# First stage of a Fourier-convolution block: PSUM tiles by half group instead of by row tile, and nine of sixteen copies on ScalarE

## The chip, the cores and the metric

The kernel runs on one core of one Trainium2 chip. The metric is the device time of one launch in microseconds (us). The engines are named as in the profile: PE (TensorE, matmuls; PEld its weight loads), DVE (VectorE), ACT (ScalarE), POOL (GpSimd), SP (SyncE, which issues DMAs).

## What is computed

One block with two parts. The first is a gated long convolution over 2048 positions and 512 channels, done by a Fourier transform; the second is a small MLP. Cut to what matters:

```python
def _A_ref(q, k, v, shift_k, ssm_k, ssm_D):
    # k_shift: a causal convolution of k with 4 taps per channel
    kv = k_shift * v
    kv_f = rfft(pad(kv, to 2S), along the positions)
    kf_f = rfft(pad(ssm_k, to 2S))
    y = irfft(kv_f * kf_f)[:S]
    y = y + kv * ssm_D
    return q * y

h  = x + _A_ref(layernorm(x), A_k, A_v, shift_k, ssm_k, ssm_D)
h2 = h + relu(layernorm(h) @ w1) @ w2
```

## The kernel before

The program writes its order out by hand: every engine executes its instructions in the order of the source, and waits on semaphores that the framework places between engines.

The transform is split into stages of small matrices. What the case is about is **the first stage**, the function `stage1(fl, B, gb, dmul)`. It is called eight times for the convolution's filter (`kfl` into `BK`, with `dmul=dmask`, lines 373 and 413; called filter groups 0 to 7 here) and eight times for the signal kv (`xfl` into `BX`, line 419; signal groups 0 to 7). Each call is one group:

- TensorE multiplies 64-row weights (a slice of `fl`) with the 64-row tables `f1hi` and `f1lo`, the second accumulating onto the first (L308). There are two row tiles, partitions 0 to 63 and 64 to 127, that hold different channels and run side by side in the array: 8 values of `gi` x 2 tables x 2 row tiles = 32 matmuls, each writing 128 columns, as runs of 32.
- The results go to two PSUM tiles of two banks each (`bank2`). In the kernel before, row tile 0 writes the first and row tile 1 the second, and the matmuls alternate between them.
- The tiles are read out. A filter group does it with two VectorE additions of the mask `dmask` (L320, the `i=0` half of the output, where the convolution's direct term is added) and two ScalarE copies (L323, the `i=1` half); where two engines read the same tile, the second waits for the first. A signal group does it with one copy of a whole tile by ScalarE and one by VectorE (`copy("AD"[rp], ...)`, in the helper's lines L278 and L280).

All these PSUM tiles come from one pool, `psum`, of four buffers that are given out in turn; so a matmul into a new tile waits until the readers of the tile allotted four before it are done. The taps' matmuls (`pkv`, L340, multiplied into `vT` by VectorE, L343), the transposes (`pst`, L291, copied by ScalarE L295 or VectorE L297) and the next stage's products draw from the same pool.

The order of the work around it: four transposing steps of the filter; then for filter groups 0 to 6 the taps of one or two row groups, the group, and some sines on ScalarE (`more_sines`, `ec_sins`); then four transposing steps of kv (`to_rows(vT, h, xfl)`), filter group 7, the eight signal groups, and the next stage, which multiplies both transforms:

```python
FIRST = "u0K +u0 u1K +u1 s0K1 s0X1 u0X s0K2 =u0 u1X =u1 ..."
```

There `u0K` is TensorE's product for one pair of frequencies from `BK` (L456), `+u0` ScalarE's copy of it (`ktu`, L442), `s0K1` and `s0X1` the same for sums, from `BK` and `BX` (`us`, L478), `u0X` the pair from `BX`, into the other half of the PSUM tile that `+u0` has read, and `=u0` VectorE's multiplication (L494). `s0X1` is the first to read `BX`, and reads from all eight signal groups. Then follow the inverse transform (`psi`, L603, whose results L278 and L280 copy too) and the MLP (L706, L722).

Of the kernel before, what the change touches and what calls it, by code (L numbers as in the profile page):

```python
# [9 lines left out]
ALU = mybir.AluOpType  # L10
BF16 = mybir.dt.bfloat16
# [4 lines left out]
P = 128  # L16
# [40 lines left out]
def kernel(  # L57
# [13 lines left out]
    nc = tc.nc  # L71
    _, S, D = A_q.shape
# [4 lines left out]
    DC = D // P  # L77
# [3 lines left out]
    halves = (lo, hi)  # L81
# [9 lines left out]
    early = pl.push("early", side="right")  # L91
# [35 lines left out]
    for dp in range(2):  # L127
        src = bass.AP(tensor=A_ssm_D.tensor, offset=A_ssm_D.offset, ap=[[0, 1], [1, DC * P]])
# [22 lines left out]
    def bank2(name):  # L151
        return psum.tile([P, 2, 512], F32, tag="ps", name=name)[:]
# [18 lines left out]
    f1hi = early.tile([P, 2, 2, 16, 2], BF16, name="f1_hi")  # L171
    f1lo = early.tile([P, 2, 2, 16, 2], BF16, name="f1_lo")
# [44 lines left out]
    for rg in range(DC):  # L217
        rows = slice(32 * rg, 32 * rg + 32)
# [21 lines left out]
    def big_sin(out, turns, scale):  # L240
        nc.scalar.activation(out=out, in_=turns, func=ACT.Sin, scale=scale * TURN / 8192)

    dmask = early.tile([P, 2, 2, 16, 2, DC], BF16, name="dmask")
    nc.gpsimd.memset(dmask[:], 0.0)
    for dp in range(2):
        row = slice(64 * dp, 64 * dp + 1)
        for rp in range(2):
            for sp in range(2):
                src = draw[row, 256 * rp:256 * rp + 256].rearrange("p (r u s l d) -> p r u s l d", r=2, s=2, l=2, d=2)[:, :, :, sp, :, dp]
                for w in range(2):  # L250
                    nc.gpsimd.tensor_copy(out=dmask[row, rp, sp, :, w].rearrange("p u (r l) -> p r u l", l=2), in_=src)

    nc.gpsimd.tensor_scalar(out=r2, in0=r2, scalar1=n2c[:], scalar2=2048.0, op0=ALU.mult, op1=ALU.add)

# [21 lines left out]
    def copy(eng, o, i):  # L276
        if eng == "A":
            nc.scalar.copy(out=o, in_=i)  # L278
        else:
            nc.vector.tensor_copy(out=o, in_=i)  # L280
# [16 lines left out]
                nc.vector.tensor_single_scalar(out=oi, in_=pst.bitcast(I32).rearrange("p b i c -> p b c i"),  # L297
                                               scalar=0, op=ALU.bitwise_or)

    def stage1(fl, B, gb, dmul=None):  # L300

        j, sp = gb // 2, gb % 2
        pss = [bank2("ps1").rearrange("p b (a w r l x) -> p (b a) (w r) l x", a=2, w=2, r=2, l=2) for _ in range(2)]
        for gi in range(8):
            g = 16 * j + 4 * (gi // 2) + 2 * sp + gi % 2
            for f, first in ((f1hi, True), (f1lo, False)):
                for rp, rows in enumerate(halves):
                    nc.tensor.matmul(out=pss[rp][:, gi // 2, :, gi % 2, :],  # L308
                                     lhsT=fl[rows, 2 * g:2 * g + 2, :].rearrange("p d n -> p (d n)"),
                                     rhs=f[rows].rearrange("p w r v h -> p (w r v h)"), start=first, stop=not first,  # L310
                                     tile_position=(64 * rp, 0), skip_group_check=True)
        o = [B.rearrange("p i (u w) (v s) x -> p i u w v s x", w=2, s=2)[:, :, 4 * j:4 * j + 4, :, :, sp, 4 * rp:4 * rp + 4]
             .rearrange("p i u w v x -> p i (u w) v x") for rp in range(2)]
        pv = [p.rearrange("p u (w r) l (v i) -> p i (u w) v (r l)", w=2, i=2) for p in pss]
        if dmul is None:
            for rp in range(2):
                copy("AD"[rp], o[rp], pv[rp])
            return
        for rp in range(2):
            nc.vector.tensor_tensor(out=o[rp][:, 0], in0=pv[rp][:, 0],  # L320
                                    in1=dmul[:, rp, sp, 4 * j:4 * j + 4].rearrange("p u w x -> p (u w) x").unsqueeze(2)
                                    .to_broadcast([P, 8, 16, 4]), op=ALU.add)
            nc.scalar.copy(out=o[1 - rp][:, 1], in_=pv[1 - rp][:, 1])  # L323

    for h in range(4):
        to_rows(sk, h, kfl)
# [38 lines left out]
    for gb in range(7):  # L365
        if gb == 3:
            taps(1, 1, 1, 1)
        elif gb < 6:
            taps(gb // 2, gb % 2)
        else:  # L370
            taps(3, 0)
            taps(3, 1, 1)
        stage1(kfl, BK, gb, dmask)
        if gb < 2:
            more_sines(gb)
        if gb == 1:
            ec_wrap(0)
        if gb in (2, 3, 4, 5):
            ec_sins(0, (gb - 2,))
# [30 lines left out]
    xfl = xkp.tile([P, P, 64], BF16, name="xfl")  # L410
    for h in range(4):
        to_rows(vT, h, xfl[:])
    stage1(kfl, BK, 7, dmask)

    BXt = bxp.tile([P, 32, 66, DC * 2], F32R, tag="X", name="BX")
    BX = BXt[:, :, 2:66, :].rearrange("p g (i k) x -> p i g k x", i=2)
    BXs = BXt[:, :, 0:32, :]
    for gb in range(8):
        stage1(xfl, BX, gb)
    pl.pop("xkp")  # L420
    pl.pop("early")

# [78 lines left out]
    for c in range(8):  # L501
        units, early = {}, {}
        for step in (OTHER if c else FIRST).split():
# [6 lines left out]
            u = step[:2]  # L510
# [296 lines left out]
```

## Time and profile before

| | |
|---|---|
| median of 3 runs | 206.26 us (206.26 to 206.31) |
| profiled execution, its own time | 206.31 us |
| its span, first to last instruction | 204.2 us |
| granted TensorE clock, mean | 0.994 |
| busy share of the span | PE 96%, PEld 67%, DVE 69%, ACT 56%, POOL 39% |
| chain that ended last, by engine | PE 88%, DVE 7%, ACT 2%, issue 1% |
| of it, first-stage matmuls (L308) | 7% of the span |
| taps (L340), next stage (L478, L456) | 5%; 9% and 7% |

A row of the page's groups, or of the timeline, gives line, engine, operation, tiles (written from read), shapes, count, and busy or elapsed time; what stands in brackets in the timeline is how long the engine was idle before and what ended that. "PE" times come from pipelined matmuls, so a busy TensorE need not be at its peak. In the chain of waits each row is a start, a length and the work that the end of the program waited for at that moment; "issue" is time in which the profile shows no reason.

### The profile page before, as it was taken

What the parts mean: (1) busy time and instruction counts of PE and PEld (TensorE: products, weight loads), DVE (VectorE), ACT (ScalarE), POOL (GpSimd) and SP (SyncE); (2) the same over time, 40 slices, a digit from 0 to 9 for tenths busy, and PEclk for the clock granted to TensorE, in tenths of its full rate; (3) what the DMA queues carried; (4) which work ended last, traced back from release to release, by engine and by line L of the source; (5) the groups of instructions that cost most, each with busy time, mean ns of one, the idle gap of its engine ahead of it and who ended that gap; (6) DMA issues with size and microseconds to landing.
All of it is one profiled execution on the core that took longest, in us unless ns stands there. A gap on an engine that the chain in (4) does not pass through costs nothing.

```text
span 204.2 us, 4733 instructions
## 1 busy us (share of the span) xinstructions
PE 195.3 (96%) x1929; PEld 137.2 (67%) x1929; DVE 141.0 (69%) x246; ACT 114.7 (56%) x188; POOL 79.6 (39%) x127
## 2 busy tenths in 40 slices
PE   8899999898999999999999999999999999999991
PEld 2475556887899999899998844475445844444460
DVE  4999888698799998997561967995378660360131
ACT  4987875788578877686880088205940164026300
POOL 7969999960559995212003032062002200002000
PEclk9999999999999999999999999999999999999997
DMA  6999990002600000052636999997643605110011
GB/s 178 337 178 207 176 176 3 3 5 31 248 3 0 3 3 0 22 132 55 106 87 184 207 215 196 171 174 91 91 82 76 135 19 103 32 58 17 0 51 51
DMA packets 47300, 19.94 MB, mean 98 GB/s; under 512 B 42186, under 2 KB 45744, under 8 KB 47280
## 3 DMA queue, kind: packets, MB, share of 16 engines
q1 hardware_dynamic: 43616, 16.14, 41.7%
q10 hardware_dynamic: 3664, 3.51, 6.0%
q8 instruction: 15, 0.25, 0.5%
q14 instruction: 5, 0.04, 0.1%
HBM read 7.02 MB, written 2.10 MB: 45 GB/s over the span
## 4 chain that ended last, share of the span: by engine, by line
PE 88%; DVE 7%; ACT 2%; issue 1%; DVEq 0%
PE ps1m L706 19%; PE ps2m L722 19%; PE psi L603 11%; PE us L478 9%; PE pz L694 7%; PE u L456 7%; PE ps L308 7%; PE pkv L340 5%; PE psz L157 2%; PE pst L291 1%; DVE E L343 1%; DVE BK L320 1%; DVE G L227 1%; DVE E L44 1%; DVE G L225 1%
## 5 line engine op out<-in xcount | busy, mean ns | idle before, releaser
L708 ACT ACTIVATE M<-ps1m 128x512 bf16<-128x512 f32 (+1 forms) x44 | 25.1, 595 | 49.4 <-PE ps1m L706 39.0
L722 PE MATMUL ps2m<-M 128*128 128x512 bf16 (+3 forms) x187 | 38.7, 366 | 0.0
L722 PEld LDWEIGHTS <-M 128*128 128x128 bf16 (+1 forms) x187 | 18.3, 98 | 19.9
L706 PEld LDWEIGHTS <-w 128*128 128x128 bf16 (+1 forms) x176 | 17.4, 100 | 19.9
L565 POOL TENSOR_SCALAR rstd<-mv 128x4 f32<-128x4 f32 x8 | 2.2, 277 | 70.1 <-DVE mv L563 70.1
L402 POOL TENSOR_TENSOR smc<-st 64x256 fp32r<-64x256 f32 x32 | 22.8, 732 | 12.4 <-PE us L478 11.5
L724 DVE SCALAR_TENSOR_TENSOR M<-ps2m,rstd,M 128x512 bf16<-128x512 f32 (+1 forms) x13 | 9.2, 707 | 24.8 <-PE ps2m L722 16.3
L494 DVE TENSOR_TENSOR BK<-u,ktu 128x512 fp32r<-128x512 f32 x32 | 21.2, 685 | 3.5 <-ACT ktu L442 1.9
L603 PE MATMUL psi<-inv,BK 128*128 128x128 f32 x128 | 21.1, 255 | 0.0
L442 ACT COPY ktu<-u 128x512 f32<-128x512 f32 x32 | 18.0, 592 | 5.2 <-PE u L456 4.2
L603 PE MATMUL psi<-inv,BX 128*128 128x256 f32 x64 | 20.5, 337 | 0.0
L603 PEld LDWEIGHTS psi<-inv,BK 128*128 128x128 f32 x128 | 19.7, 197 | 0.0
L706 PE MATMUL ps1m<-M,w 128*128 128x512 bf16 (+1 forms) x88 | 19.3, 379 | 0.0
L706 PE MATMUL ps1m<-xT,w 128*128 128x512 bf16 (+1 forms) x88 | 19.3, 379 | 0.0
L478 PE MATMUL us<-BK,smc 64*128 64x256 f32 x128 | 14.5, 302 | 0.6 <-ACT BX L278 0.6
L456 PE MATMUL u<-BK,st 64*128 64x256 f32 x128 | 13.6, 290 | 0.2 <-DVE BX L494 0.2
L478 PE MATMUL us<-BX,smc 64*128 64x256 f32 x128 | 13.3, 282 | 0.0
L323 ACT CAST BK<-ps 128x512 fp32r<-128x512 f32 x16 | 9.4, 586 | 6.6 <-PE ps L308 4.9
L456 PE MATMUL u<-BX,st 64*128 64x256 f32 x128 | 13.0, 281 | 0.0
L603 PEld LDWEIGHTS psi<-inv,BX 128*128 128x128 f32 x64 | 12.1, 196 | 0.3 <-DVE BK L494 0.3
L561 DVE BATCH_NORM_STATS2 st<-M 128x6 f32<-128x512 bf16 x20 | 12.3, 676 | 0.0
L494 DVE TENSOR_TENSOR BX<-us,kts 128x512 fp32r<-128x512 f32 x16 | 11.0, 686 | 0.8 <-ACT kts L442 0.5
(132 smaller groups left out, 407.2 us busy)
## 6 DMA issues: line engine op xcount, KB each, us to landing
E<-in_A_ssm_k_dram SPq DMA_DIRECT2D x1, 2048.0 KB
out_dram<-M ACTq DMA_DIRECT2D x15, 128.0 KB
w<-in_B_w_dram SPq DMA_DIRECT2D x1, 1376.0 KB
M<-in_B_w_dram ACTq DMA_DIRECT2D x1, 1280.0 KB
M<-in_A_q_dram SPq DMA_DIRECT2D x8, 128.0 KB
xh<-in_A_q_dram SPq DMA_DIRECT2D x4, 128.0 KB
xr<-in_A_q_dram SPq DMA_DIRECT2D x4, 128.0 KB
out_dram<-M ACTq DMA_DIRECT2D x2, 64.0 KB
```

The source lines that it names most:

```text
L308: nc.tensor.matmul(out=pss[rp][:, gi // 2, :, gi % 2, :], lhsT=fl[rows, 2 * g:2 * g + 2, :].rearrange("p d n -> p (d n)"), rhs=f[rows].rea ...
L402: nc.gpsimd.tensor_tensor(out=smc[pq, c % 3, i, :, 64 * dp:64 * dp + 64], in0=st[pq, ks, 64:128].bitcast(F32), in1=st[pq, ks, 0:64].bitcas ...
L442: nc.scalar.copy(out=kt[:], in_=ps)
L456: nc.tensor.matmul(out=ps[:, dp, 256 * x:256 * x + 256], lhsT=t[pq], rhs=cols((BK, BX)[x], pq, k1, i), start=not begun, stop=(i == 1), til ...
L478: mm = nc.tensor.matmul(out=ps[:, k % 2, 256 * x:256 * x + 256], lhsT=smc[pq, k // 4 % 3, i, k % 4, :], rhs=cols((BK, BX)[x], pq, k, i), s ...
L494: nc.vector.tensor_tensor(out=o, in0=ps[:, :, 256:512].rearrange("p b (g x) -> p b g x", x=8), in1=kt[:].rearrange("p b (g x) -> p b g x", ...
L561: nc.vector.bn_stats(out=st[:, i, :], in_=src[:, i, :])
L603: nc.tensor.matmul(out=o if part == 0 else o[:, P * part - P:P * part], lhsT=src[:, g // 2, :, g % 2::2].rearrange("p c r -> p (c r)"), rh ...
L694: nc.tensor.matmul(out=pz[:, i, :, a:a + w, :].rearrange("p (s r) a n -> p s r (a n)", s=2), lhsT=ax[rho][:, n2 // 2, n2 % 2, :], rhs=ecor ...
L706: nc.tensor.matmul(out=ps1[:fsz, :].rearrange("p (i t) -> p i t", i=4), lhsT=w1[:, c, fc * P:fc * P + fsz], rhs=hT[sc][:, :, c, :], start= ...
L708: nc.scalar.activation(out=h1T[:fsz, fc, :], in_=ps1[:fsz, :], func=ACT.Relu)
L722: nc.tensor.matmul(out=ps2, lhsT=h1T[:ksz, fc, i * P:(i + 1) * P], rhs=w2[:ksz, fc, d0:d0 + w], start=(fc == 0), stop=(fc == NFC - 1))
```

## The change

The two PSUM tiles of a group are cut another way. Each tile now holds half of the group's `gi` values (four of eight) for both row tiles; the row tile picks the bank inside the tile. TensorE fills the first tile with 16 matmuls and then the second with 16, and takes the second tile only then. In PSUM the columns stand in another order, so that the output's eight last elements are one step of 128 elements apart across the two banks, and each reader writes runs of eight elements where it wrote runs of four.

Filter groups are read with the same four instructions of the same size, now by half (VectorE half 0, ScalarE half 1, then VectorE half 1, ScalarE half 0). `dmask` is laid out to match; GpSimd fills it with the same 16 copies. Signal groups are read with two copies for each tile (one for each `i`) where there was one, both on one engine: `engs` names the engine of each half. Groups 0 to 3 have ScalarE on the first half and VectorE on the second, group 4 has ScalarE on both, groups 5 to 7 VectorE on the first and ScalarE on the second: nine tiles of 16 on ScalarE, seven on VectorE.

```diff
-    dmask = early.tile([P, 2, 2, 16, 2, DC], BF16, name="dmask")
+    dmask = early.tile([P, 2, 16, 2, 2 * DC], BF16, name="dmask")
...
-                    nc.gpsimd.tensor_copy(out=dmask[row, rp, sp, :, w].rearrange("p u (r l) -> p r u l", l=2), in_=src)
+                    nc.gpsimd.tensor_copy(out=dmask[row, sp, :, w, 4 * rp:4 * rp + 4].rearrange("p u (r l) -> p r u l", l=2), in_=src)
...
-    def stage1(fl, B, gb, dmul=None):
+    def stage1(fl, B, gb, dmul=None, engs="AD"):
...
         j, sp = gb // 2, gb % 2
-        pss = [bank2("ps1").rearrange("p b (a w r l x) -> p (b a) (w r) l x", a=2, w=2, r=2, l=2) for _ in range(2)]
-        for gi in range(8):
-            g = 16 * j + 4 * (gi // 2) + 2 * sp + gi % 2
-            for f, first in ((f1hi, True), (f1lo, False)):
-                for rp, rows in enumerate(halves):
-                    nc.tensor.matmul(out=pss[rp][:, gi // 2, :, gi % 2, :],
-                                     lhsT=fl[rows, 2 * g:2 * g + 2, :].rearrange("p d n -> p (d n)"),
-                                     rhs=f[rows].rearrange("p w r v h -> p (w r v h)"), start=first, stop=not first,
-                                     tile_position=(64 * rp, 0), skip_group_check=True)
-        o = [B.rearrange("p i (u w) (v s) x -> p i u w v s x", w=2, s=2)[:, :, 4 * j:4 * j + 4, :, :, sp, 4 * rp:4 * rp + 4]
-             .rearrange("p i u w v x -> p i (u w) v x") for rp in range(2)]
-        pv = [p.rearrange("p u (w r) l (v i) -> p i (u w) v (r l)", w=2, i=2) for p in pss]
-        if dmul is None:
-            for rp in range(2):
-                copy("AD"[rp], o[rp], pv[rp])
-            return
-        for rp in range(2):
-            nc.vector.tensor_tensor(out=o[rp][:, 0], in0=pv[rp][:, 0],
-                                    in1=dmul[:, rp, sp, 4 * j:4 * j + 4].rearrange("p u w x -> p (u w) x").unsqueeze(2)
-                                    .to_broadcast([P, 8, 16, 4]), op=ALU.add)
-            nc.scalar.copy(out=o[1 - rp][:, 1], in_=pv[1 - rp][:, 1])
+        todo = []
+        for half in range(2):
+            ps = bank2("ps1")
+            pw = ps.rearrange("p b (r l a w x) -> p b a l w r x", r=2, l=2, a=2, w=2)
+            for gi in range(4):
+                g = 16 * j + 8 * half + 4 * (gi // 2) + 2 * sp + gi % 2
+                for f, first in ((f1hi, True), (f1lo, False)):
+                    for rp, rows in enumerate(halves):
+                        nc.tensor.matmul(out=pw[:, rp, gi // 2, gi % 2],
+                                         lhsT=fl[rows, 2 * g:2 * g + 2, :].rearrange("p d n -> p (d n)"),
+                                         rhs=f[rows].rearrange("p w r v h -> p (w r v h)"), start=first, stop=not first,
+                                         tile_position=(64 * rp, 0), skip_group_check=True)
+            us = slice(4 * j + 2 * half, 4 * j + 2 * half + 2)
+            o = [B[:, i].rearrange("p (u w) (v s) x -> p u w v s x", w=2, s=2)[:, us, :, :, sp]
+                 .rearrange("p u w v x -> p (u w) v x") for i in range(2)]
+            pv = [ps.rearrange("p b (y m v i) -> p i m v (b y)", m=4, y=4, i=2)[:, i] for i in range(2)]
+            if dmul is None:
+                for i in range(2):
+                    copy(engs[half], o[i], pv[i])
+                continue
+            dm = dmul[:, sp, us].rearrange("p u w x -> p (u w) x").unsqueeze(2).to_broadcast([P, 4, 16, 8])
+            todo.append((lambda o=o, pv=pv, dm=dm: nc.vector.tensor_tensor(out=o[0], in0=pv[0], in1=dm, op=ALU.add),
+                         lambda o=o, pv=pv: copy("A", o[1], pv[1])))
+        if dmul is not None:
+            for half, i in ((0, 0), (1, 1), (1, 0), (0, 1)):
+                todo[half][i]()
...
-        stage1(xfl, BX, gb)
+        stage1(xfl, BX, gb, engs="AA" if gb == 4 else "DA" if gb > 4 else "AD")
```

## The prediction, made before the changed kernel was run

> **What bounds the kernel now.** I read the page first. The profiled execution took 206.31 us, its span 204.2 us, so 2.1 us lie around the span, which the change doesn't touch. The median of the three runs is 206.26 us, 0.05 us below; the sum below is made against 206.31. The measurement can tell about 0.2% (0.41 us) from no change.
>
> ```profile
> span 204.2 us, 4733 instructions
> PE 195.3 (96%) x1929; PEld 137.2 (67%) x1929; DVE 141.0 (69%) x246; ACT 114.7 (56%) x188; POOL 79.6 (39%) x127
> ```
>
> TensorE (PE) looks full at 96%, but that is an average. Next I read the busy times by stretch, with cuts where the chain of waits leaves TensorE (start and end, length, then each engine's busy time):
>
> ```profile
> core 0: us, PE busy (x) PEld busy (x) DVE busy (x) ACT busy (x) POOL busy (x), PEclk, DMA share, GB/s
> 23.10:34.40 11.30, 11.30 (x163) 6.63 (x163) 9.12 (x12) 8.01 (x10) 10.46 (x19) 1.00 0.81 106
> 34.40:40.60 6.20, 5.54 (x128) 5.24 (x127) 4.62 (x7) 4.81 (x8) 5.91 (x9) 1.00 0.01 3
> 40.60:49.95 9.35, 8.54 (x233) 7.36 (x232) 9.30 (x8) 8.10 (x9) 3.46 (x5) 1.00 0.03 6
> 49.95:84.60 34.65, 34.44 (x508) 32.41 (x508) 30.34 (x49) 26.22 (x48) 23.07 (x23) 1.00 0.13 42
> ```
>
> TensorE has no gap at all in 23.1 to 34.4 and nearly none from 49.95 on. It loses 0.66 us in 34.4 to 40.6, and in 40.60 to 49.95, where the eight signal groups of the first stage stand, it is VectorE (DVE) that is busy 9.30 of 9.35 us. The granted clock is 1.00 in all of them. The chain of waits (start, length, what) shows both places, and one more ahead of 23.1:
>
> ```profile
> 22.45 0.59 ACT BK L323
> 23.05 0.04 issue
> 23.09 1.05 PE ps L308 x31
> ...
> 28.81 1.00 PE ps L308 x32
> ...
> 38.19 1.06 PE ps L308 x31
> ...
> 41.77 1.20 PE ps L308 x32
> ...
> 48.80 1.01 ACT BX L278
> 49.81 0.14 issue
> 49.95 0.76 PE us L478 x8
> ```
>
> A group is 32 matmuls in 1.00 us where nothing holds it. Call the two PSUM tiles of a group a and b. PSUM has four such tiles, given out in turn, so each tile waits until the tile four before it is read out.
>
> **Place 1, filter group 3.** The timeline has the first matmuls of this group and of the last filter group (7), group 7's readers, VectorE's last products with the taps and two copies of transposed rows:
>
> ```profile
> 22.37 0.23 PE L308 MATMUL ps<-f_hi,E 64*128 64x128 bf16 x1
> ...
> 31.69 2.42 DVE L343 TENSOR_TENSOR E<-pkv,E 128x1024 bf16<-128x1024 f32 x3 [0.42 <-PE pkv L340]
> ...
> 37.12 1.50 ACT L295 COPY xfl<-pst 128x1024 f32<-128x1024 f32 x2 [0.48 <-PE pst L291]
> 37.79 0.22 PE L308 MATMUL ps<-f_hi,E 64*128 64x128 bf16 x1
> 38.01 0.69 DVE L297 TENSOR_SCALAR xfl<-pst 128x512 int32<-128x512 int32 x1 [0.55 <-PE pst L291]
> 39.24 1.35 DVE L320 TENSOR_TENSOR BK<-ps,dmask 128x512 fp32r<-128x512 f32 x2 [0.54 <-PE ps L308]
> 39.28 1.27 ACT L323 CAST BK<-ps 128x512 fp32r<-128x512 f32 x2 [0.65 <-PE ps L308]
> ```
>
> In the kernel before, matmuls for a and b alternate, so at 22.37 one matmul goes into a and the next, for b, waits for ScalarE's (ACT) copy that ends at 23.04. All 31 others stand behind it. In the changed order, 16 matmuls fill a first: they run in 22.37 to 22.87, inside the wait, and b's 16 run from 23.09 to 23.59. The group ends at 23.59 and not at 24.09, so TensorE gains 0.5 us. What is late next? The taps' matmuls behind it need b of group 2, which VectorE reads beside ScalarE's copy, on the other tile, and leaves about as that ends; after that TensorE is without a gap up to 34.4, so the whole stretch moves 0.5 us ahead. VectorE and ScalarE have 2.2 and 3.3 us free in it, and VectorE's products that read the transposing DMAs' rows wait for TensorE, not for a DMA (the row at 31.69). I take 0.5, from 0 (VectorE is late, or a DMA lands under 0.5 us ahead of its reader) to 0.5.
>
> The evictions of the filter groups do not change in count or size: two VectorE additions and two ScalarE copies of 128x512 in each group. ScalarE's first copy still needs b, VectorE's second still follows it on the same tile, so their end stays 1.3 us behind the group's end. VectorE's first addition could begin 0.5 us sooner, but the taps' product occupies it then; worth nothing. The mask's 16 GpSimd copies keep their 64 elements: nothing.
>
> **Place 2, filter group 7.** Everything comes 0.5 us earlier: a's matmuls at 37.3 to 37.8. b stalled from 37.8 to 38.19 for the first of ScalarE's two copies at 37.12; that copy comes 0.5 sooner too, so b's run in 37.8 to 38.3 with no stall. The signal groups need VectorE's last transposed rows, 38.70 before, 38.2 now. So the first signal tile is filled from 38.3 to 38.8. Evictions of group 7: VectorE on a from 38.15 (free then) to 38.83; ScalarE on b 38.42 to 39.0, then on a 38.92 to 39.51; VectorE on b to 39.73. ScalarE is free for the signal tiles at 39.42 and VectorE at 39.64.
>
> **Place 3, the signal groups.** The two engines' work there, and the step behind it:
>
> ```profile
> 40.45 1.02 ACT L278 CAST BX<-ps 128x1024 fp32r<-128x1024 f32 x1
> 40.50 9.55 DVE L280 CAST BX<-ps 128x1024 fp32r<-128x1024 f32 x8
> 41.69 2.14 ACT L278 CAST BX<-ps 128x1024 fp32r<-128x1024 f32 x2 [0.22 <-PE ps L308]
> 49.70 1.08 ACT L442 COPY ktu<-u 128x512 f32<-128x512 f32 x2
> 50.51 0.45 PE L456 MATMUL u<-BX,st 64*128 64x256 f32 x4
> ```
>
> VectorE reads eight tiles without a break, (9.55 - 1.22)/7 = 1.19 us each, and ends at 50.05; ScalarE, at about 1.0 us a tile, waits for TensorE, which waits for VectorE's tiles. The change replaces each 128x1024 copy by two of 128x512: 18 on ScalarE, 14 on VectorE. The nearest rows are the casts of the inverse stage, also f32 to fp32r, out of two banks with 8 elements in a run and the same 128-element step in PSUM:
>
> ```profile
> 87.42 0.59 ACT L278 CAST ax<-psi 128x512 fp32r<-128x512 f32 x1
> 87.90 0.60 ACT L278 CAST BX<-psi 128x512 fp32r<-128x512 f32 x1
> ...
> 97.27 0.68 DVE L280 CAST BX<-psi 128x512 fp32r<-128x512 f32 x1
> 97.87 0.68 DVE L280 CAST ax<-psi 128x512 fp32r<-128x512 f32 x1
> ```
>
> ScalarE's starts lie 0.48 apart, and the ktu copies' 1.08 - 0.59 = 0.49, although each lasts 0.59: the next starts before the last has ended. VectorE's lie 0.60 apart at 0.68. So the price is the pace: 0.485 x 18 = 8.7 us on ScalarE and 0.605 x 14 = 8.5 us on VectorE, where before VectorE needed 9.5. The row at 37.12 is a 1024 and a 512 copy in 1.50, so a large one has a pace of 1.50 - 0.59 = 0.91; splitting costs ScalarE 2 x 0.48 - 0.91 = 0.05 us a tile and VectorE 2 x 0.60 - 1.19 = 0.01. Bounds: ScalarE 0.455 (half of 0.91) to 0.59 (no overlap), VectorE 0.595 to 0.68. I take the rows' own paces, same operation and same pattern.
>
> The Trainium skill (Perfetto Trace Analysis, Optimizing Scalar/DVE Operations) speaks against the split: it asks for larger operations where an engine is saturated, and gives an overhead per instruction from PSUM of about 51 ns for ScalarE and 125 ns for VectorE. ScalarE's 0.05 us agrees; VectorE's 0.01 does not. With 0.125, VectorE's seven tiles would take 9.2 us, end near 48.9, and the time would be about 205.3, a case that lies with rival 3 below; I go by the rows.
>
> Does TensorE keep up? A half is 16 matmuls, 0.50 us, readable about 0.1 us after the last issue. From the starts above, ScalarE's tiles end at 40.50 and every 0.97 us after, VectorE's at 40.93 and every 1.21 us. With four tiles in turn each half is filled just in time; from the fifth ScalarE tile on some come 0.02 to 0.05 us late. In group 4 ScalarE takes both tiles, and VectorE's next is filled at 44.5, as it comes free. ScalarE's last copy ends at 39.42 + 17 x 0.485 + 0.59 = 48.26, with the lateness 48.35; VectorE's at 48.2 to 48.3. Before, 49.80 and 50.05.
>
> Behind ScalarE's last copy stand its copies of the first two products (ktu), which the next matmuls into the same tile wait for. The first then ends at 48.25 + 0.59 = 48.84, and TensorE's step that started at 50.51 can start at 48.9. The steps ahead of it (s0's two parts, 50.51 - 49.95 = 0.56 us) wait for the last VectorE tile: 48.3 + 0.6 = 48.9 too. The gain is 50.51 - 48.9 = 1.6 us: 0.5 from place 1, some 0.5 from place 2, and 0.6 from place 3. From there on TensorE has 34.44 of 34.65 us and the tail is the same work, so all of it moves ahead: 206.31 - 1.6 = 204.7 us.
>
> **The rivals.**
> 1. *ScalarE's copies don't overlap here.* At 0.587 each, as the duration says, 18 take 10.6 us, from 39.42 to 50.0; ktu ends at 50.6 and the step starts at 50.65, 0.14 later than before: 206.45, no change. For it: the copies' own waits for TensorE could break the overlap. Against it: the casts above at 0.48 and ktu's two copies at 0.49, both with waits. The Trainium skill (VectorE: DVE Perf Modes, The TRN2 errata) has a rule of this kind: a ScalarE copy out of PSUM takes 172 cycles and one per element at 1.2 GHz, 570 ns for 512. By it, as a pace, ScalarE would end at 49.7 and the time would be about 206.1; the durations of 0.59 agree with it and the paces of 0.48 don't. Chance 0.10, with what lies within 0.2%.
> 2. *ScalarE becomes the bound, and slower than VectorE was.* It has 18 copies and the ktu copies behind them. The pace from which it decides is (50.51 - 0.05 - 0.59 - 39.42)/18 = 0.58 us. Should reading 8 elements across two banks while TensorE fills others cost 0.65, 18 take 11.7, the step starts at 51.75: 207.5, slower. For it: ScalarE's share is the larger one, 9 of 16. Against it: the same pattern at 0.48 in the inverse stage, also beside matmuls. Chance 0.09.
> 3. *Only part of it is gained.* If place 1 is taken back (VectorE is busy 9.12 of 11.30 us there), the gain is 1.1; if halves come late, since a stall now costs TensorE 0.2 us in a signal group (1.20 at 41.77 against 1.00) and there are twice as many places to stall, 0.2 to 0.7 less. 205.2 to 205.9. Chance 0.21.
> 4. *The change doesn't do what it says:* the framework could make the first matmul wait for both tiles. The built order speaks against it: b's wait stands 32 instructions behind a's. It would leave place 3, near 205.7, and is counted with 3.
>
> **How the numbers follow.** The forecast, 204.2 to 205.2 about 204.7, has 0.60; its low end, and the range's, is 0.15 lower with VectorE at 0.595 (14 x 0.01) and ScalarE at 0.455, 0.2 with the 0.21 us gone that TensorE idles in 49.95 to 84.6, and 0.1 with no half late: 204.2. Rival 3 has 0.21, rival 1 0.10, rival 2 0.09. Faster by over 0.2% is 0.81, within 0.2% 0.10, slower 0.09. The range 204.2 to 206.0 leaves out rival 2 and most of rival 1, under 2 in 10.
>
> **What would show it.** In the profile after: filter group 3's stall is only half a group long, and the taps behind it start near 23.6; the first signal matmul is at 38.3; ScalarE's casts in the signal groups have starts 0.48 to 0.50 apart, VectorE's 0.60; both end near 48.3; the first us matmuls follow at once, the u step on BX starts near 48.9, and all that follows stands 1.6 us earlier. The prediction is wrong if ScalarE's starts lie 0.58 or more apart, if either engine idles over 0.1 us at each tile, or if the gain at 23.6 is gone at 34.

## The result, and the profile after

| | before | changed |
|---|---|---|
| median | 206.28 us (6 runs, 206.26 to 206.61) | 205.23 us (6 runs, 204.87 to 205.30) |
| profiled execution, its span | 206.31, 204.2 us | 205.23, 203.1 us |
| ratio to before | | 0.9943, 95% interval 0.993 to 0.9956 |

The changed kernel is faster: by the ratio 0.57% (0.44 to 0.70%), and the medians lie 1.05 us apart. Forecast were 204.7 us, a gain of 1.6, and the range 204.2 to 206.0. The way and the order of size were right; 0.5 us of the gain is missing in the profile, and one row names it.

The busy times by stretch of the changed kernel, the last two cuts moved to where its chain has them:

```profile
core 0: us, PE busy (x) PEld busy (x) DVE busy (x) ACT busy (x) POOL busy (x), PEclk, DMA share, GB/s
23.10:34.40 11.30, 10.85 (x147) 6.18 (x147) 9.78 (x14) 8.27 (x11) 10.11 (x18) 1.00 0.74 97
34.40:40.60 6.20, 6.09 (x150) 5.82 (x149) 4.58 (x7) 5.15 (x9) 5.91 (x9) 1.00 0.01 3
40.60:48.83 8.23, 7.44 (x220) 6.50 (x215) 8.08 (x14) 8.23 (x18) 3.51 (x5) 1.00 0.05 8
48.83:83.53 34.70, 34.47 (x508) 32.41 (x508) 30.29 (x48) 26.36 (x49) 23.03 (x23) 1.00 0.12 42
```

From 34.4 to 40.6 TensorE loses 0.11 us and not 0.66. In the signal groups ScalarE has no gap (8.23 of 8.23) and VectorE nearly none (8.08): both bound the stage, where VectorE alone did. But 23.1 to 34.4 now has a gap of 0.45 us; in the kernel before, the wait of 0.49 us for the same tile stood just ahead of 23.1. The timeline of the changed kernel, in the order of time:

```profile
23.55 0.23 PE L312 MATMUL ps<-f_hi,E 64*128 64x128 bf16 x2 [0.57 <-ACT BK L278]
38.89 0.23 PE L312 MATMUL ps<-f_hi,xfl 64*128 64x128 bf16 x2
39.90 8.93 ACT L278 CAST BX<-ps 128x512 fp32r<-128x512 f32 x18
40.17 8.51 DVE L280 CAST BX<-ps 128x512 fp32r<-128x512 f32 x14
48.83 0.51 PE L485 MATMUL us<-BK,smc 64*128 64x256 f32 x4 [0.41 <-DVE BX L280]
49.39 0.50 PE L463 MATMUL u<-BX,st 64*128 64x256 f32 x4
```

The u step on BX, 50.51 before, starts at 49.39: 1.12 us sooner, which is the gain of the span. Group 3's second tile is filled from 23.55, not from 23.09. The row that explains it is VectorE's wrap of phases, L269, in the queue ahead of that tile's readers. First the kernel before, VectorE, GpSimd and the taps behind group 3, then the changed one, with the readers of that tile:

```profile
20.01 0.68 DVE L269 TENSOR_SCALAR G<-G 128x1024 int32<-128x1024 int32 x1
19.41 1.85 POOL L353 TENSOR_SCALAR G<-E,wf 128x512 f32<-128x512 bf16 x2
21.34 1.27 POOL L356 TENSOR_TENSOR G<-G 128x512 f32<-128x512 f32 x1
24.07 1.90 PE L340 MATMUL pkv<-F,E 128*128 128x512 bf16 x8
```

```profile
20.00 1.16 DVE L269 TENSOR_SCALAR G<-G 128x1024 int32<-128x1024 int32 x1
19.25 1.36 POOL L360 TENSOR_SCALAR G<-E,wf 128x512 f32<-128x512 bf16 x2
20.69 1.59 POOL L363 TENSOR_TENSOR G<-G 128x512 f32<-128x512 f32 x1
22.21 1.27 DVE L325 TENSOR_TENSOR BK<-ps,dmask 128x512 fp32r<-128x512 f32 x2
22.91 0.59 ACT L278 CAST BK<-ps 128x512 fp32r<-128x512 f32 x1 [0.83 <-DVE BK L325]
24.11 1.90 PE L347 MATMUL pkv<-F,E 128*128 128x512 bf16 x8
```

Before, L269 took 0.68 us and GpSimd's two instructions beside it 1.85; in the changed kernel 1.16 and 1.36. The sums are 2.53 and 2.52: one of the two waits 0.48 us for the other. (GpSimd's next instruction, beside the end of L269, then took 1.59 and not 1.27, so here both lose.) GpSimd's pair began 0.16 us sooner in the changed kernel; that so little decides which one waits is a reading, not shown. L269 is not touched by the change. Behind it VectorE's additions of group 2 run from 22.21, ScalarE's copy on the same tile ends at 23.50 where it ended at 23.04, and the taps start at 24.11, no sooner than before.

### The profile page after: what moved, and what is told of

It is laid out like the page before. It is cut to its first block, busy times and chain, and to the rows that moved or that the text cites. A ratio compares the mean times of both kernels' runs of the same rounds, so it can differ in the third digit from the quotient of the medians.

```text
span 203.1 us, 4751 instructions
## 1 busy us (share of the span) xinstructions
PE 194.7 (96%) x1929; PEld 136.9 (67%) x1929; DVE 140.3 (69%) x252; ACT 115.1 (57%) x198; POOL 79.3 (39%) x127
## 4 chain that ended last, share of the span: by engine, by line
PE 73%; DVE 1%; ACT 0%; issue 0%
PE ps1m L713 19%; PE ps2m L729 19%; PE psi L610 11%; PE us L485 9%; PE pz L701 7%; PE u L463 7%; PE pm L533 1%; DVE BX L280 0%; DVE BX L501 0%; ACT kts L449 0%; DVE M L731 0%; DVE ax L280 0%
## 5 line engine op out<-in xcount | busy, mean ns | idle before, releaser
L687 DVE TENSOR_TENSOR qT<-pz,qT 128x2048 bf16<-128x2048 f32 x2 | 4.6, 2290 | 10.6 <-DMA qT<-M 6.5
```

## The experiments

Theory P: the half-group order, the paces and the shares do what the prediction says, and 0.48 us was lost to L269, which waits for GpSimd. Rival Q: half-group order is worth nothing in the filter groups. Rivals R and S are about the signal groups: the share of the engines alone makes the gain, or the share is worth nothing without half tiles. The ratios stand against the kernel before on the same chip; its median was 206.43, 206.40 and 206.35 us in the three sessions.

### The wrap one group later

```diff
-        if gb == 1:
+        if gb == 2:
             ec_wrap(0)
```

> The changed kernel, with VectorE's wrap of the cosine-sine phases (L269) moved one group later, behind filter group 2's additions. Theory P (the 0.5 us of place 1 was lost because L269 took 1.16 us at 20.00, beside GpSimd, and not 0.68, and stood ahead of the reads that free group 3's second tile): that tile comes free near 22.9 and not at 23.5, and the time is 204.7 to 204.8 us. Rival Q (TensorE's half-group order gives nothing in the filter groups whatever VectorE does): 205.2, as the changed kernel.

Measured: 204.93 us (204.72 to 205.26), ratio 0.9924 (0.9911 to 0.9937). Four runs lie at 204.72 to 204.97, the profiled one at 205.26. Its timeline:

```profile
23.00 0.23 PE L312 MATMUL ps<-f_hi,E 64*128 64x128 bf16 x2
23.55 1.90 PE L347 MATMUL pkv<-F,E 128*128 128x512 bf16 x8
26.37 2.05 SPq L138 DMA_TRANSPOSE E<-in_A_v_dram  x1
26.58 1.23 DVE L350 TENSOR_TENSOR E<-pkv,E 128x1024 bf16<-128x1024 f32 x1 [0.52 <-PE ps L312]
31.74 2.42 DVE L350 TENSOR_TENSOR E<-pkv,E 128x1024 bf16<-128x1024 f32 x3 [0.38 <-DMA E<-in_A_v_dram]
```

The second half runs from 23.00 and the taps from 23.55, as forecast for place 1. But in this execution the transposing DMAs were late: the last was issued at 26.37, in the kernel before at 25.27. VectorE's product at 26.58 stood at 26.01 before; the row names TensorE, but the taps that it multiplies had ended at 25.45, so it waited for something else, probably a DMA (not shown). The last products, at 31.74, released by TensorE before, waited for the last DMA. The 0.5 us was gained at 23.6, and the products had lost it by 26.6; at 34 nothing of it was left. The other four runs fit P within 0.2 us.

### Even shares

```diff
-        stage1(xfl, BX, gb, engs="AA" if gb == 4 else "DA" if gb > 4 else "AD")
+        stage1(xfl, BX, gb, engs="AD")
```

> The changed kernel with the signal groups' tiles shared evenly, eight to ScalarE and eight to VectorE. Theory P with the paces of the prediction: VectorE reads 16 halves at 0.60 us, ends near 49.9 instead of 48.7, TensorE's first step on BX comes about 0.9 us later: 206.0 to 206.1 us. Rival (half tiles alone give the gain in the signal groups, the share of the engines nothing): 205.2.

Measured: 205.63 us (205.23 to 205.71), ratio 0.9954 (0.9941 to 0.9967). The rows:

```profile
39.82 8.57 ACT L278 CAST BX<-ps 128x512 fp32r<-128x512 f32 x16
40.09 9.65 DVE L280 CAST BX<-ps 128x512 fp32r<-128x512 f32 x16
50.03 0.41 PE L463 MATMUL u<-BX,st 64*128 64x256 f32 x4
```

VectorE reads 16 halves in 9.65 us and ends at 49.74, as expected; the step behind it came 0.6 us later and not 0.9, and 206.0 to 206.1 was too much. So the share is worth some 0.4 us in the medians and 0.6 at the step. What is left of the gain without it doesn't come from the signal groups: the kernel with half tiles in the filter groups only, below, has the same ratio within the noise (0.996).

### One copy for each signal tile

```diff
             if dmul is None:
-                for i in range(2):
-                    copy(engs[half], o[i], pv[i])
+                copy(engs[half], B.rearrange("p i (u w) (v s) x -> p i u w v s x", w=2, s=2)[:, :, us, :, :, sp]
+                     .rearrange("p i u w v x -> p i (u w) v x"), ps.rearrange("p b (y m v i) -> p i m v (b y)", m=4, y=4, i=2))
                 continue
```

> The changed kernel with one copy of 128x1024 for each signal tile instead of two of 128x512; tiles, order and shares stay. By paces of 0.92 us on ScalarE and 1.19 on VectorE, ScalarE ends near 48.3 (48.8 in the changed kernel) and VectorE near 48.5 (48.7): 205.0 us, a gain of 0.1 to 0.2 since VectorE then ends last. Rival (a tile is freed and read in finer steps with two copies, and this is worth more than an instruction's overhead): 205.3 or more.

Measured: 204.60 us (204.35 to 204.67), ratio 0.9905 (0.9892 to 0.9918), better than either expected. Its timeline:

```profile
39.83 8.45 ACT L278 CAST BX<-ps 128x1024 fp32r<-128x1024 f32 x9
40.10 8.12 DVE L280 CAST BX<-ps 128x1024 fp32r<-128x1024 f32 x7
48.37 0.51 PE L485 MATMUL us<-BK,smc 64*128 64x256 f32 x4 [0.44 <-DVE BX L280]
48.92 0.45 PE L463 MATMUL u<-BX,st 64*128 64x256 f32 x4
```

With last durations of 1.04 and 1.22 us the paces are (8.45 - 1.04)/8 = 0.93 and (8.12 - 1.22)/6 = 1.15. Two copies cost (8.93 - 0.59)/17 x 2 = 0.98 and (8.51 - 0.68)/13 x 2 = 1.20. The split costs each engine 0.05 us a tile; the changed kernel pays it nine times on ScalarE and, beside that, seven times on VectorE, and the u step on BX comes 0.47 us sooner without it (48.92 after 49.39). The Trainium skill (Perfetto Trace Analysis, Optimizing Scalar/DVE Operations) asks for larger operations on a saturated engine: this run agrees. Of its overheads, ScalarE's 51 ns agrees with 0.05 and VectorE's 125 ns does not.

### Filter groups that alternate

```diff
+        if dmul is not None:       # both tiles are taken first
+            for gi in range(4):
+                for half in range(2):
+                    fill_half(both[half], half, gi)
```

> The changed kernel, but in the filter groups alone both tiles are taken at once and TensorE's matmuls alternate between the two halves, as they alternated between row tiles before. Theory P: the 0.5 us that half a group does inside the wait in group 3, and the part of a stall in group 7, are lost: 205.6 to 205.8 us. Rival Q (the filter groups' order gives nothing): 205.2.

Measured: 205.52 us (205.45 to 205.92), ratio 0.9955 (0.9942 to 0.9968). The interval overlaps the changed kernel's 0.993 to 0.9956, so alone it settles nothing. In the profile ScalarE's first signal copy starts at 40.35 and not at 39.90:

```profile
40.35 8.92 ACT L278 CAST BX<-ps 128x512 fp32r<-128x512 f32 x18
```

The other half is the kernel with half tiles in the filter groups only, below.

### The changed kernel again

> The changed kernel as it is, for comparison on the same chip with the three others. 204.9 to 205.3 us, as in its first runs; by theory P the runs near 204.9 are those in which the wrap L269 is not held up by GpSimd.

Measured: 205.25 us, ratio 0.9929 (0.9915 to 0.9943). The five runs are 204.82, 204.88, 205.25, 205.25 and 205.32: two values, 0.4 us apart. In the profiled one (205.32) L269 took 1.22 us:

```profile
19.32 1.36 POOL L360 TENSOR_SCALAR G<-E,wf 128x512 f32<-128x512 bf16 x2
20.02 1.22 DVE L269 TENSOR_SCALAR G<-G 128x1024 int32<-128x1024 int32 x1
```

No run near 204.85 was profiled.

### The share alone

```diff
-                copy("AD"[rp], o[rp], pv[rp])
+                copy(engs[rp], o[rp], pv[rp])
...
-        stage1(xfl, BX, gb)
+        stage1(xfl, BX, gb, engs="AA" if gb == 4 else "DA" if gb > 4 else "AD")
```

(in the kernel before)

> The kernel before (tiles by row tile, matmuls that alternate, copies of 128x1024), with nothing changed but the engines of the signal tiles: nine on ScalarE, seven on VectorE, in the changed kernel's order. Theory P: VectorE has 7 x 1.19 = 8.3 us and ScalarE 9 x 0.92 = 8.3, in place of VectorE's 9.5, but both tiles of a group come free for TensorE together and it stalls in the middle, so some 0.6 of the 1.2 us arrives: 205.7 us. Rival R (the share alone makes the whole gain): 205.2 or less. Rival S (the share is worth nothing without half tiles): 206.3.

Measured: 207.06 us (206.62 to 207.21), ratio 1.0025 (1.0015 to 1.0034): slower, outside all three expectations. Eight of the eleven runs lie at 207.01 to 207.21 and three, the profiled one among them, at 206.62 to 206.66; the kernel before had 6 of 15 at 206.59 to 206.88 and most others at 206.27 to 206.40. So like compared with like the loss is some 0.35 us, and the rest of the medians' 0.66 is the larger number of runs at the upper value. The rows show why it is slower, and L269 in a profile at the lower value:

```profile
19.28 1.87 POOL L353 TENSOR_SCALAR G<-E,wf 128x512 f32<-128x512 bf16 x2
19.99 0.68 DVE L269 TENSOR_SCALAR G<-G 128x1024 int32<-128x1024 int32 x1
40.44 1.02 ACT L278 CAST BX<-ps 128x1024 fp32r<-128x1024 f32 x1
40.49 4.81 DVE L280 CAST BX<-ps 128x1024 fp32r<-128x1024 f32 x4
46.41 1.22 DVE L280 CAST BX<-ps 128x1024 fp32r<-128x1024 f32 x1 [1.10 <-PE ps L308]
48.21 2.36 DVE L280 CAST BX<-ps 128x1024 fp32r<-128x1024 f32 x2 [0.57 <-PE ps L308]
44.05 3.98 ACT L278 CAST BX<-ps 128x1024 fp32r<-128x1024 f32 x4 [0.22 <-PE ps L308]
50.96 0.41 PE L456 MATMUL u<-BX,st 64*128 64x256 f32 x4
```

With tiles by row tile TensorE needs both tiles of the next group before it can finish either. ScalarE's double turn in group 4 holds both, VectorE stands idle for 1.10 and 0.57 us, and its saved tile of 1.2 us is more than lost. R falls, and S is right in that the share alone gains nothing.

The signal groups by themselves, from ScalarE's first signal copy to the u step on BX in each profile, leave out what L269 and the DMAs do ahead of them:

| tiles, copies of a tile, share | first copy | u step | us |
|---|---|---|---|
| row tile, one, 8 to 8 (kernel before) | 40.45 | 50.51 | 10.06 |
| row tile, one, 9 to 7 | 40.44 | 50.96 | 10.52 |
| half, two, 8 to 8 | 39.82 | 50.03 | 10.21 |
| half, two, 9 to 7 (changed kernel) | 39.90 | 49.39 | 9.49 |
| half, one, 9 to 7 | 39.83 | 48.92 | 9.09 |

Neither part gains here alone, at the copies tried: the two need each other. Half tiles at 8 to 8 with one copy a tile were not tried.

### Without GpSimd's taps

```diff
-    taps_gpsimd(1, 3)
```

> The changed kernel without GpSimd's taps (one row group of 512 positions is left without its convolution with the four taps; eight GpSimd instructions of 0.7 to 1.3 us between 19 and 28 us are gone). Theory P, that VectorE's wrap L269 is held up by GpSimd's work beside it: L269 takes 0.68 us in this profile (at most 0.9, for what GpSimd then does in that place is short), group 3's second half starts near 23.1, and the time is 204.6 to 204.8. Rival (L269 is slow because of ScalarE's sines, which read the same tile from 20.00 on, or because of the DMA): it takes 1.1 as before, 205.2.

Measured: 204.90 us (204.81 to 204.99), ratio 0.9919 (0.9905 to 0.9932), no run near 205.25; P had 204.6 to 204.8.

```profile
20.20 0.77 DVE L269 TENSOR_SCALAR G<-G 128x1024 int32<-128x1024 int32 x1
20.36 0.78 POOL L390 TENSOR_TENSOR E<-E 128x64 f32<-128x64 f32 x1
23.36 0.23 PE L312 MATMUL ps<-f_hi,E 64*128 64x128 bf16 x2 [0.18 <-ACT BK L278]
```

L269 takes 0.77 us, with ScalarE's sines beside it as before. So GpSimd's work and not the sines held it up. (GpSimd's L390, which now stands beside it, took 0.78 us; in the first experiment, away from it, 0.32.) The Trainium skill (Perfetto Trace Analysis, Optimizing Scalar/DVE Operations) says that the two engines share an SBUF read port, which a VectorE operation on two ports holds as a lock. The sums of 2.53 and 2.52 us agree with that; the port itself no run shows.

### Both edits that gained

The later wrap and the single copy together.

> The changed kernel with the two edits that gained: one copy of 128x1024 for each signal tile, and the wrap L269 behind filter group 2. If their gains are of separate stages, 0.45 and 0.3 add: 204.3 us. If the wrap's gain is limited by the DMA transposes (the profile of the kernel with the later wrap had VectorE wait for them at 26.58 and 31.74), 204.4 to 204.6.

Measured: 204.15 us (204.11 to 204.44), ratio 0.9886 (0.9872 to 0.9899): the two gains add, and this is the fastest version, 1.1 us below the changed kernel. It is also 0.45 us below the kernel with the single copy alone, from which it differs only in where L269 stands.

### Half tiles in the filter groups only

```diff
+    def stage1(fl, B, gb, dmul=None):
+        (stage1_row if dmul is None else stage1_half)(fl, B, gb, dmul)
```

(`stage1_half` is the changed function, `stage1_row` that of the kernel before.)

> Half tiles in the filter groups alone; the signal groups as in the kernel before (tiles by row tile, one copy each of 128x1024, eight to each engine). Theory P: the filter groups' order gives what the kernel with alternating filter groups lost, some 0.5 to 0.6 us where the wrap L269 is not held up: 205.7 to 205.8 us in such runs, 206.1 to 206.2 in the others. Rival Q (the order of the filter groups is worth nothing): 206.3 and 206.7, as before.

Measured: 205.58 us (205.42 to 206.01), ratio 0.996 (0.9947 to 0.9973). Q falls: the order of the filter groups is worth 0.4% (0.27 to 0.53%) by itself. Here L269 took 0.71 us, and the timeline shows the gain and its limit:

```profile
23.66 1.90 PE L375 MATMUL pkv<-F,E 128*128 128x512 bf16 x8
29.33 3.63 PE L375 MATMUL pkv<-F,E 128*128 128x512 bf16 x16
31.44 2.42 DVE L378 TENSOR_TENSOR E<-pkv,E 128x1024 bf16<-128x1024 f32 x3 [0.58 <-DMA E<-in_A_v_dram]
39.82 1.01 ACT L278 CAST BX<-ps 128x1024 fp32r<-128x1024 f32 x1
```

The taps at 23.66 stood at 24.07 before; but VectorE's last products start at 31.44 after 31.69, only 0.25 us sooner, because now the DMA releases them.

### The kernel before with the later wrap

The edit of the first experiment, in the kernel before.

> The kernel before with VectorE's wrap L269 behind filter group 2, as in the kernel with the later wrap. Theory P' (the times of the kernel before lie about two values, 206.3 and 206.7, because VectorE's wrap does or does not wait for GpSimd): its runs lie about one value, 206.1 to 206.3, with none near 206.7. Rival (the two values come from the transposing DMAs or from another stage): they stay.

Measured: ten of twelve runs at 206.17 to 206.30 us, two at 207.55 and 207.64 that nothing here explains (their granted clock is 0.992, that of the ten 0.997 to 1.0); ratio 1.0 (0.9985 to 1.0016). Beside it, the kernel before had 4 of 17 runs at 206.65 to 206.89. None of the twelve lies there, which fits P': those runs would be the ones in which L269 waits. None of them was profiled, so this is inferred.

## Why the prediction was right, and where it was too high

- **Place 1 (0.5 us forecast): nothing arrived in the profiled execution.** The taps, forecast near 23.6, start at 24.11 (24.07 before). Half of group 3 did run inside the wait. What failed is the step "the next, for b, waits for ScalarE's copy that ends at 23.04": it took that end from one trace as if VectorE's queue ahead of it were fixed. L269 stood there with 0.68 us and took 1.16, the copy ended 0.46 later, and TensorE waited until 23.55. With the wrap moved, and with half tiles in the filter groups alone, where L269 took 0.71, the taps start at 23.55 and 23.66, as forecast. The prediction also named a DMA that lands late as the other limit, and the gain at 23.6 being gone at 34 as a sign that it is wrong. This limit took all of the 0.5 in the profile with the later wrap and 0.15 of 0.4 us with half tiles in the filter groups alone. The sum took 0.5, the top of its own range of 0 to 0.5, and that was too much also without L269.
- **Place 2 (0.5 us): right.** ScalarE came free for the signal tiles 0.55 us sooner (39.90 after 40.45), without place 1. b's stall is gone: TensorE runs from 37.82 through group 7 without a wait.
- **Place 3 (0.6 us): right, to the row.** ScalarE's pace was 0.49 (forecast 0.485), VectorE's 0.60 (0.605); the spans of 18 and 14 copies were 8.93 and 8.51 us. From ScalarE's first signal copy to the u step on BX the prediction had 48.9 - 39.42 = 9.48 us; measured 49.39 - 39.90 = 9.49.
- **The price of the split on VectorE was wrong.** The prediction had 0.01 us a tile, from a pace of 1.19 for a full copy. That average holds waits: in "The share alone" VectorE's last two full copies, one right behind the other, take 2.36 us, a pace of 2.36 - 1.22 = 1.14, and the split costs 2 x 0.60 - 1.14 = 0.06. This term isn't in the forecast's sum, which goes by the halves' own pace; it is why the single copy did better than expected.
- **The sum.** By place the u step gained -0.04, 0.59 and 0.57 us, together 1.12; forecast were 0.5, 0.5 and 0.6. That 1.6 less L269's 0.48 is 1.12 too is in part luck. The whole of it reached the end. The runs of the changed kernel near 204.85 would be those without that loss; this is inferred from the experiments on L269, since none of them was profiled. They too lie above 204.7.
- **The rivals.** No overlap of ScalarE's copies (0.59 a copy): wrong, their starts lie 0.49 apart though one lasts 0.65 on average. ScalarE slower than VectorE was: wrong. Part of the gain only: this is what the median shows, by the path named there, place 1 taken back on VectorE, though of the two sizes named (1.1 and less) it is the first. The median of 205.23 lies in this rival's band, 205.2 to 205.9, and 0.03 us outside the forecast's own.
- **The rule of the Trainium skill** against the split (Perfetto Trace Analysis, Optimizing Scalar/DVE Operations) was right in kind (0.05 to 0.06 us a tile on each engine) and was rightly not decisive: half tiles with the new share gain more than the split costs, and without the split they gain most.

## What to carry to other kernels

Where matmuls alternate between two buffers, the wait for the second stops the first too; filling one buffer and then the other puts half the work inside the wait. Shifting readout work between engines only pays once the buffers come free one at a time: in the signal groups the same 9 to 7 share gained 0.72 us on half tiles (10.21 to 9.49) and lost 0.46 us on tiles that are needed in pairs (10.06 to 10.52). Before a gain is booked at a wait, look at the queue ahead of its releaser for an instruction whose time hangs on another engine.

## What the runs showed of the hardware that was not expected

- A VectorE int32 operation from SBUF to SBUF (L269, 1024 elements, 0.68 us) and GpSimd's operations held each other up: L269 took 1.16 and 1.22 in the two profiles of the changed kernel, or GpSimd's pair took 1.85 and not 1.36. VectorE's products from PSUM beside GpSimd kept their 1.20 to 1.23 us.
- A full copy's pace was the same out of both kinds of tile, whether the output is written in runs of eight elements or of four, once waits are left out. Out of the tiles by row tile, the first row below (the share alone on ScalarE) gives (2.84 - 1.03)/2 = 0.91 us, and the row at 48.21 further up 1.14 on VectorE. Out of the half tiles, the other two (the single copy) give (4.68 - 1.05)/4 = 0.91 and (3.49 - 1.21)/2 = 1.14. Averages over longer rows, 0.99 and 1.19, hold waits.

```profile
45.18 2.84 ACT L278 CAST BX<-ps 128x1024 fp32r<-128x1024 f32 x3
43.60 4.68 ACT L278 CAST BX<-ps 128x1024 fp32r<-128x1024 f32 x5
44.73 3.49 DVE L280 CAST BX<-ps 128x1024 fp32r<-128x1024 f32 x3
```
